# Units 4 to 15 of a recurrence plus gated MLP: outputs, scores and carry in one TensorE visit, on five banks, in a re-searched order

## The chip, the cores and the metric

One core of one Trainium2 chip runs the whole program. The metric is device microseconds of one execution; less is better. The kernel before took 556.14 us (median of three runs, 554.99 to 556.77).

## The reference

A gated linear recurrence over 768 steps for 4 batches of 8 heads with 48 channels each, and then a gated MLP on its output, laid out as 3072 tokens of 384 features (d_ff 1536):

```python
for t in range(S):
    state = alpha[:, :, t, :, None] * state + np.einsum('bhd,bhe->bhde', k[:, :, t], v[:, :, t])
    y[:, :, t] = np.einsum('bhd,bhde->bhe', q[:, :, t], state)
...
g = x @ w_gate
silu = g * (1.0 / (1.0 + np.exp(-g)))
val = x @ w_val
return (silu * val @ w_out).astype(np.float32)
```

## The kernel before

**The recurrence** runs in 16 units of 192 steps, four units to a batch, each of three chunks of 64 steps (`C`, `NU`). The eight heads stand in four groups `g` of two; one head of a group has its channels on partitions 0 to 47, the other on 64 to 111. VectorE scans alpha into decays (`G`, `f`), k and q are scaled by them (`mk`, `q`), and TensorE then does three small jobs per unit, all in f32:

- *scores* (`S`, line 551): k times q inside each chunk, 24 matmuls of 48 rows by 64 columns into two banks. They take turns over all four 64 by 64 quarters of the array: for `f` = 0 rows low to columns high and rows high to columns low, for `f` = 1 low to low and high to high.
- *carry* (`B`, line 575): what each chunk adds to the state, 24 matmuls with 64 rows and 48 columns (16 in the last unit of a batch), all but four of them in one bank. They take turns over two quarters only: rows high to columns low, rows low to columns high.
- *outputs* (`Y`, lines 647, 648 and 664): 36 matmuls, in two banks, 12 over all rows and 24 over quarters. They need the masked scores (`ma`) and the carried states of all chunks (`ad`), which VectorE makes after scores and carry of the same unit.

In the records each of these f32 matmuls is two. For the carry, k is turned to rows by VectorE (`kr`, line 526, eight transposes of 32 by 384 a unit, into one buffer `K`); v is loaded by six DMAs a unit, one for each chunk and parity of head (`V`, line 434); for two of the four groups it is copied once more into `U` (`vc`, line 497). The outputs leave their banks twice: rounded to fp32r on ScalarE (`yh`, line 678) and the rest by VectorE (`yl`, line 682), two of each a unit, and DMAs (`xr`, line 718) put them in the MLP's input `xT`.

**The MLP** runs in eight blocks of 384 tokens, two units to a block, by twelve steps of 128 hidden features: 96 steps `s`, each with a gate product `g`, a value product `v` and an output product `o` of nine matmuls of 128 by 128 by 384 each (lines 733 and 765). `g` has one bank (`gps`), `v` one (`vps`), `o` three (`ops0` to `ops2`). ScalarE takes the gate (`sl`) and rounds (`hh`), VectorE multiplies (`h`), GpSimd or VectorE takes the rest (`hl`). The weights come as 64-bit floats and are cut to f32 pairs by VectorE, ScalarE and GpSimd (`wNv0` to `wNp`) until some 200 us; blocks 0 and 1 are done in two halves of features for that.

**What sets the order:** the string `ORDER`. Each word is an engine letter (t TensorE, v VectorE, s ScalarE, g GpSimd, y the DMA issues of SyncE), a task, and after `@` the banks, by their place in `BANKS` (0 to 2 `A0` to `A2`, 3, 4, 7 `ops0` to `ops2`, 5 `vps`, 6 `gps`). Each engine runs its words in that order; semaphores do the rest. Scores and carry stand side by side; the outputs of the unit before stand next to them in six cases of twelve and elsewhere in the other six.

Of the kernel before, what the change touches and what calls it, by code (L numbers as in the profile page):

```python
# [8 lines left out]
F32 = mybir.dt.float32  # L9
F32R = mybir.dt.float32r  # L10
# [7 lines left out]
P = 128  # L18
# [33 lines left out]
s:x0.0 s:x0.1 s:x0.2 t:Tq2@17 s:cq2 s:w2a g:w2p y:V3.3 y:V2.3 y:wl13 y:V2.5 y:V2.2 y:V2.4 y:Lq3 y:V2.1 v:yl1.0
t:R1.1@2 s:x1.1 v:w4v2 t:Tk2@07 v:mk2 v:f2 t:R1.2@6 t:R1.0@0 s:pk3 s:x1.2 s:x1.0 s:w3a v:w3p v:q2 t:K2.0@4 t:K2.1@7
s:kc2.0 s:kc2.1 t:g0 s:sl0 y:wl5 v:de2 s:w4a t:Tk3@04 t:K2.2@2 s:ea3 t:g1 s:kc2.2 s:qc2 s:sl1 s:w5v0 s:pq3 y:V3.1
v:w4p v:G3 t:v0 v:h0 s:hh0 g:lm0 g:hl0 t:g2 t:C2.0@2 s:ad2.0 t:S2@13 s:sl2 t:C2.1@5 s:ad2.1 v:w5v1 v:mk3 t:Tq3@26
s:cq3 v:f3 t:K3.0@4 g:q3 t:K3.1@7 t:C2.2@0 s:kc3.0 s:kc3.1 s:ad2.2 v:w6v0 t:v1 v:ma2.2 v:lm1 v:ma2.1 v:ma2.0 y:wl12
# [12 lines left out]
y:V5.0 y:os6.1 v:kr4.3 v:kr4.1 v:tq5 t:v13 t:S4@02 t:B4@1 v:w18v0 s:ad4.0 v:h13 y:Lk6 y:V5.4 v:ad4.1 t:o11 t:o12
v:ad4.2 s:hh13 v:qc4 g:hl13 t:g14 v:ma4.0 v:f5 v:ma4.2 v:w16v2 v:w17v1 s:sl14 t:v14 v:h14 t:o13 s:ot13.0 s:ot13.1  # L70
y:os13.1 y:V5.3 y:La6 s:hh14 v:w18v1 v:hl14 v:w18v2 t:g15 s:sl15 t:v15 v:w17v2 s:w16a g:w16p t:g16 v:h15 s:hh15 g:hl15
v:vc4 v:ma4.1 g:q5 s:w17a s:sl16 g:w18a g:w17p y:os13.0 y:wl19 y:pl18.2 y:V5.2 v:kr5.0 t:v16 v:h16 t:g17 s:sl17
v:kr5.1 s:ot13.2 v:tr6 t:v17 t:o14 v:h17 s:hh17 t:Y4@56 g:hl17 g:w18p s:yh4.0 s:w19v0 s:yh4.1 v:tk6 v:kr5.3 v:kr5.2
t:o15 t:S5@10 t:B5@2 v:yl4.1 t:g18 s:sl18 v:yl4.0 v:w19v1 v:G6 v:mk6 v:kr6.2 t:v18 s:hh16 g:hl16 v:w19v2 v:h18 t:g19
s:w19a g:w19p g:qc5 t:o16 s:sl19 s:hh18 g:hl18 v:f6 v:kr6.3 t:v19 v:h19 t:o17 s:hh19 g:hl19 t:o18 t:g20 s:sl20 v:ma5.0
v:de5 v:ma5.1 v:ma5.2 v:ot18.2 y:os13.2 y:wr8 y:Lq6 v:kr6.1 y:xr4.0 y:La7 y:V6.3 y:V6.5 y:xr4.2 v:tq6 y:xr4.1 g:q6
t:v20 v:h20 y:V6.4 y:pl18.1 t:g21 s:hh20 g:hl20 v:ad5.0 v:ad5.1 v:ad5.2 s:vc5 s:sl21 t:v21 v:h21 t:Y5@07 s:yh5.0
y:os18.2 y:V6.1 y:wr19 y:V6.0 y:pl18.0 y:V6.2 y:Lk7 t:g22 v:tr7 y:Lq7 s:yh5.1 s:sl22 v:ot18.1 v:yl5.0 v:kr6.0 v:yl5.1
v:ot18.0 y:xr5.0 y:xr5.1 y:xr5.2 y:os18.0 y:os18.1 t:v22 v:h22 t:S6@21 t:B6@0 t:g23 t:o19 t:o20 s:hh22 g:hl22 v:G7
t:v23 s:hh21 v:f7 v:tk7 v:hl21 t:o21 t:o22 s:sl23 g:mk7 g:qc6 v:h23 v:kr7.1 v:kr7.2 v:kr7.0 v:de6 v:ad6.0 v:ma6.0  # L80
# [101 lines left out]
def main_path(ctx, tc, q, k, v, alpha, w_gate, w_val, w_out, out, flag, spill):  # L182
# [483 lines left out]
    def rows_of(u, i, x):  # L666
        return state[u]["Y"][0:112, x, i::2, :].bitcast(F32R), state[u]["yps"][i][0:112]
# [461 lines left out]
```

## Time and profile before

| | |
|---|---|
| median of three runs | 556.14 us |
| the profiled execution | 557.46 us |
| its span, first to last instruction | 555.6 us |
| granted clock of TensorE, mean | 0.998 |
| busy: TensorE, VectorE, ScalarE, GpSimd | 536.7, 392.0, 253.4, 146.0 us |

Busy time of TensorE counts overlapping records once, and matmuls overlap: one of 337 ns starts 173 ns after the one ahead of it. What a matmul costs the stream is therefore read from the distance between starts, not from its length.

### The profile page before, as it was taken

To read this page: it belongs to the slowest core of one execution; us is meant where nothing else is said; L and a number is where in the kernel's file an instruction comes from. 1 tells how busy PE (TensorE), PEld (TensorE's weight loads), DVE (VectorE), ACT (ScalarE), POOL (GpSimd) and SP (SyncE) were. 2 spreads that over 40 slices of the span, in tenths; PEclk is the share of its full clock that TensorE was granted. 3 is DMA by queue.
4 is the path that set the end of the run, shared out by engine and by line. 5 is a ranking of instruction groups with operands and counts; after the bars stand their busy time and mean duration, and the time that the engine had idled before them with its cause. 6 is when DMAs were issued, how large, how long until landed. Compare 5 with 4: busy or idle time off the path is not lost.

```text
span 555.6 us, 13364 instructions
## 1 busy us (share of the span) xinstructions
PE 536.7 (97%) x5350; PEld 521.0 (94%) x5350; DVE 392.0 (71%) x614; ACT 253.4 (46%) x576; POOL 146.0 (26%) x151
## 2 busy tenths in 40 slices
PE   5899999998999999999999999999999999999996
PEld 4788999998989999999999999999999999999996
DVE  7989998999998997775878559786856332321222
ACT  6888755333223223242332434217243335447775
POOL 7313326626415340112311232142130101001100
PEclk9999999999999999999999999999999999999999
DMA  8979479542576856434247535744361213244453
GB/s 252 267 192 305 134 211 236 148 104 85 148 184 167 196 132 148 109 96 101 75 111 193 136 89 133 154 113 139 90 173 30 67 39 92 81 127 126 127 178 99
DMA packets 95361, 77.59 MB, mean 140 GB/s; under 512 B 32832, under 2 KB 92224, under 8 KB 95296
## 3 DMA queue, kind: packets, MB, share of 16 engines
q1 hardware_dynamic: 95008, 76.32, 51.5%
q8 instruction: 43, 0.70, 0.6%
q10 hardware_dynamic: 288, 0.39, 0.2%
q14 instruction: 22, 0.18, 0.1%
HBM read 62.52 MB, written 5.90 MB: 123 GB/s over the span
## 4 chain that ended last, share of the span: by engine, by line
PE 72%; DVE 13%; DMA 5%; SPq 3%; issue 3%; ACT 2%; POOL 1%; DVEq 0%; ACTq 0%
PE v L733 22%; PE g L733 21%; PE ops L765 20%; DMA L<-in_q_dram 2%; PE y L664 2%; DVE K L526 2%; PE s L551 2%; DVE AT L469 1%; PE A L575 1%; DVE Gs L460 1%; DVE h L745 1%; DVE trk L396 1%; DMA L<-in_alpha_dram 1%; DVE AT L396 1%; PE y L647 1%
## 5 line engine op out<-in xcount | busy, mean ns | idle before, releaser
L733 PE MATMUL v<-xT,w 128*128 128x384 f32 x864 | 167.3, 337 | 2.7 <-DVE h L745 2.7
L733 PE MATMUL g<-xT,w 128*128 128x384 f32 x864 | 167.3, 337 | 0.0
L765 PE MATMUL ops<-w,hh 128*128 128x384 f32 x576 | 157.6, 336 | 0.0
L733 PEld LDWEIGHTS v<-xT,w 128*128 128x128 f32 x864 | 150.7, 188 | 4.8 <-DVE h L745 4.0
L733 PEld LDWEIGHTS g<-xT,w 128*128 128x128 f32 x864 | 150.7, 188 | 1.2 <-ACT xT L708 0.2
L754 POOL TENSOR_TENSOR hl<-h,hh 128x384 fp32r<-128x384 f32 x62 | 63.5, 1028 | 265.9 <-ACT hh L749 248.8
L745 DVE TENSOR_TENSOR h<-h,v 128x384 f32<-128x384 f32 x96 | 53.0, 552 | 101.2 <-PE v L733 97.2
L749 ACT CAST hh<-h 128x384 fp32r<-128x384 f32 x96 | 49.0, 513 | 145.5 <-PE ops L765 76.2
L765 PEld LDWEIGHTS ops<-w,hh 128*128 128x128 f32 x576 | 105.3, 188 | 0.4
L765 PE MATMUL ops<-w,hl 128*128 128x384 f32 x288 | 96.8, 336 | 0.6 <-DVE hl L754 0.6
L741 ACT ACTIVATE h<-g 128x384 f32<-128x384 f32 x96 | 46.9, 489 | 88.1 <-PE g L733 75.8
L526 DVE STREAM_TRANSPOSE K<-Gs 32x384 f32<-32x384 f32 x96 | 54.7, 570 | 2.0
L765 PEld LDWEIGHTS ops<-w,hl 128*128 128x128 f32 x288 | 54.1, 188 | 0.9 <-DVE hl L754 0.9
L754 DVE TENSOR_TENSOR hl<-h,hh 128x384 fp32r<-128x384 f32 x34 | 21.3, 629 | 23.1 <-ACT hh L749 22.9
L344 POOL TENSOR_TENSOR w<-t,w 128x768 fp32r<-128x768 f32 (+1 forms) x13 | 23.4, 1808 | 40.3 <-ACT w L340 36.2
L469 DVE TENSOR_TENSOR_SCAN AT<-AT,back 128x771 f32<-128x771 f32 x16 | 32.9, 2058 | 0.6
L460 DVE TENSOR_TENSOR_SCAN Gs<-AT,inj 128x772 f32<-128x772 f32 x16 | 28.9, 1809 | 0.1
L597 DVE TENSOR_TENSOR X<-s,mask 64x384 f32<-64x384 f32 (+1 forms) x48 | 26.1, 551 | 4.1 <-PE s L551 1.8
L678 ACT CAST X<-y 112x384 fp32r<-112x384 f32 x28 | 12.5, 477 | 27.4 <-PE y L664 21.5
L682 DVE TENSOR_TENSOR X<-y,X 112x384 fp32r<-112x384 f32 x28 | 15.2, 551 | 12.8 <-ACT X L678 12.6
L317 ACT ACTIVATE wc<-wc,wbias 128x384 f32<-128x384 f32 x36 | 23.3, 647 | 1.2
L485 POOL TENSOR_TENSOR X<-trq,AT 112x768 f32<-112x768 f32 x9 | 15.5, 1723 | 22.1 <-DVE K L526 9.8
(122 smaller groups left out, 584.9 us busy)
## 6 DMA issues: line engine op xcount, KB each, us to landing
xT<-X SPq DMA_DIRECT2D x84, 72.0 KB, 2.2
raw<-in_moe_w_gate_dram SPq DMA_DIRECT2D x12, 384.0 KB, 5.1
raw<-in_moe_w_val_dram SPq DMA_DIRECT2D x12, 384.0 KB, 5.2
V<-in_v_dram SPq DMA_DIRECT2D x96, 48.0 KB, 3.7
raw<-in_moe_w_out_dram SPq DMA_DIRECT2D x12, 384.0 KB, 5.6
wc<-in_moe_w_gate_dram SPq DMA_DIRECT2D x12, 384.0 KB, 3.8
wc<-in_moe_w_out_dram SPq DMA_DIRECT2D x12, 384.0 KB, 3.6
wc<-in_moe_w_val_dram SPq DMA_DIRECT2D x12, 384.0 KB, 3.7
```

Source lines behind the costliest of these rows:

```text
L317: nc.scalar.activation(dev, dev, AF.Relu, bias=wbias, scale=-1.0, accum_out=wviol[:, 0, i : i + 1])
L344: eng.tensor_tensor(out=lo, in0=src, in1=hi.bitcast(F32), op=ALU.subtract)
L460: nc.vector.tensor_tensor_scan(*(x.rearrange("p g t -> p (g t)")[:, ::-1] for x in (Gs, AT, inj)), 0.0, op0=ALU.mult, op1=ALU.add)
L469: nc.vector.tensor_tensor_scan(Af, Af, back[:, 1 : n + 1], back[:, 0:1], op0=ALU.mult, op1=ALU.add)
L526: nc.vector.transpose(out=bass.AP(k0.tensor, k0.offset, [k0.ap[0], (G * 2 * D, NU), (2 * D, G), (1, 32)]), in_=Kg[j * BO + x : j * BO + x ...
L597: nc.vector.tensor_tensor(out=X[r, z, f * GF : (f + 1) * GF, :].rearrange("r g (c t) -> r g c t", c=NU), in0=sps[f][r].rearrange("r g (c t ...
L733: nc.tensor.matmul(pt, wsp[kind, f][a][:, kt * P : (kt + 1) * P], xT[blk][:, b_, kt, :], start=(n == 0), stop=(n == 3 * KT - 1),)
L741: nc.scalar.activation(h, acc.pop(("g", blk, f)), AF.Silu)
L745: nc.vector.tensor_tensor(out=h, in0=h, in1=acc.pop(("v", blk, f)), op=ALU.mult)
L749: nc.scalar.copy(out=hh, in_=acc["h", blk, f])
L754: eng.tensor_tensor(out=hl, in0=acc.pop(("h", blk, f)), in1=hh.bitcast(F32), op=ALU.subtract)
L765: nc.tensor.matmul(ops[blk][i], h[b_][:, i * P : (i + 1) * P], wsp["o", f][a], start=(first and n == 0), stop=(last and n == 2),)
```

## The change

The word `Z` takes the place of `S` and `B` for units 4 to 15 and of `Y` for units 4 to 14. `Zu` issues the outputs of unit u-1, the scores of unit u and the carry of unit u, one behind the other (`Z4` has no outputs; `Y15` stays by itself). It holds five banks: one for the outputs of groups 0 and 1, two for the scores, and two (`halves`) that hold the outputs of group 2 or 3 in their first 192 columns and the carry of two groups behind them.

The carry's matmuls now take turns over four quarters, as the scores do: high to low, low to high, high to high, low to low. For that, in groups 2 and 3 the two heads have changed sides in `K` and `V`. v is loaded head by head (eight DMAs a unit in place of six); the transposes of k are halved in width and doubled in number (16 of 32 by 192); the outputs of groups 2 and 3 read `V`, so the copy `vc` is gone from unit 4 on; the outputs are evacuated in three pieces (384, 192 and 192 columns), and a chunk's states (`ad`) in four, where chunks 0 and 1 took two. Units 0 to 3 compute as before. `ORDER` is new on all engines from about unit 0's outputs on.

```diff
 ORDER = """
...
-v:de5 v:ma5.1 v:ma5.2 v:ot18.2 y:os13.2 y:wr8 y:Lq6 v:kr6.1 y:xr4.0 y:La7 y:V6.3 y:V6.5 y:xr4.2 v:tq6 y:xr4.1 g:q6
+t:Z5@12560 s:yh4.0 v:yl4.0 v:ma5.0 v:ma5.1 g:w18p t:v18 g:mk6 v:kr6.0 v:ma5.2 v:h18 v:de5 s:yh4.1 s:yh4.2 v:ad5.0
...
+            g, j = divmod(i, 2)
+            h = j if g >= GF else 1 - j
+            eng.dma_start(
+                out=Vd[h * BO : h * BO + C, :, g, VC[1 - h]],
+                in_=v[b, i, t0 : t0 + T, :].rearrange("(c s) e -> s c e", c=NU),
+            )
...
         for y in range(0, C, 32):
-            r = (1 - j) * BO + y
-            k0 = Kt_[u % NK][r : r + 32, j * D + x : j * D + x + 32]
-            nc.vector.transpose(
-                out=bass.AP(k0.tensor, k0.offset, [k0.ap[0], (G * 2 * D, NU), (2 * D, G), (1, 32)]),
-                in_=Kg[j * BO + x : j * BO + x + 32, :, :, y : y + 32],
-            )
+            for f in range(2):
+                h = j if f else 1 - j
+                r = h * BO + y
+                k0 = Kt_[u % NK][r : r + 32, f * GF * 2 * D + (1 - h) * D + x : f * GF * 2 * D + (1 - h) * D + x + 32]
+                nc.vector.transpose(
+                    out=bass.AP(k0.tensor, k0.offset, [k0.ap[0], (G * 2 * D, NU), (2 * D, GF), (1, 32)]),
+                    in_=Kg[j * BO + x : j * BO + x + 32, :, f * GF : (f + 1) * GF, y : y + 32],
+                )
...
-    def carry(u, bank, whole=False):
+    def carry(u):
...
+        cs = [t_[:, T : T + NU * GF * D].rearrange("p (c g e) -> p c g e", c=NU, g=GF) for t_ in st["halves"]]
+        st["cps"] = [[(slice(f * GF, (f + 1) * GF), cs[f][:, c]) for f in range(2)] for c in range(NU)]
         for c in range(NU - last_of_batch(u)):
...
+            for g0 in range(GF):
+                for f in range(2):
+                    for j in (1, 0) if f else (0, 1):
+                        h = j if f else 1 - j
+                        r, g = slice(h * BO, h * BO + C), f * GF + g0
                         nc.tensor.matmul(
-                            to[j * BO : j * BO + D, g - gs.start, :], Ks[r, x, g, KC[j]], Vd[r, x, g, VC[j]],
-                            start=(x == 0 or not whole), stop=(x == c),
+                            cs[f][j * BO : j * BO + D, c, g0, :], Ks[r, c, g, KC[1 - h]], Vd[r, c, g, VC[1 - h]],
+                            start=True, stop=True,
                         )
...
+            if u >= NROWS:
+                b = [
+                    (to, Vd[r, c, g, cols], X[r, 1, g, cx])
+                    for to, r, cols, g in ((y[E], lo, O, 2), (y[O], up, E, 2), (z[O], lo, O, 3), (z[lo], up, lo, 3))
+                ]
...
+    def burst(u, banks):
+
+
+        halves = [ps.tile([P, 512], F32, tag=banks[i], name=f"c{i}_{u}") for i in range(2)]
+        state[u]["halves"] = halves
+        if banks[4:]:
+            outputs(u - 1, banks[2:3], halves)
+        scores(u, banks[-2:])
+        carry(u)
```

TensorE around unit 9, before. `y_8` are the outputs of unit 8, `s_9` the banks of the scores of unit 9, `A_9` the carry's bank; `g`, `v` and `ops` rows are products of the MLP; x16 is sixteen instructions of one form in a row.

```order
L733 MATMUL v_0_3239<-xT_2680,w_424 128x384 x9
L647 MATMUL y_8_3259<-X_102,V_80 64x64
...
L664 MATMUL y_8_3260<-X_102,V_80 48x64
L733 MATMUL g_1_3324<-xT_2680,w_589 128x384 x9
...
L733 MATMUL g_5_3456<-xT_2680,w_1052 128x384 x9
L551 MATMUL s_9_3486<-X_103,Gs_2943 64x64 x2
L551 MATMUL s_9_3487<-X_103,Gs_2943 64x64 x2
...
L575 MATMUL A_9_3512<-V_81,K_104 48x48 x16
L575 MATMUL s_9_3486<-V_81,K_104 48x48 x4
L575 MATMUL A_9_3512<-V_81,K_104 48x48 x4
L765 MATMUL ops_0_0_3382<-w_964,hh_2_3417 128x384
```

The same place now, with `c_9` for the two `halves`:

```order
L760 MATMUL v_3_3457<-xT_2764,w_967 128x384 x9
L658 MATMUL y_3482<-X_102,V_80 64x64
...
L680 MATMUL c_9_3481<-X_102,V_80 48x64 x2
L680 MATMUL c_9_3480<-X_102,V_80 48x64 x2
L565 MATMUL s_9_3519<-X_103,Gs_3025 64x64 x2
L565 MATMUL s_9_3520<-X_103,Gs_3025 64x64 x2
...
L584 MATMUL c_9_3480<-V_81,K_104 48x48 x2
L584 MATMUL c_9_3481<-V_81,K_104 48x48 x2
...
L760 MATMUL g_4_3577<-xT_2764,w_1088 128x384 x9
```

Two visits between the products have become one, and the carry changes its bank, and with it its quarters, after every two matmuls.

VectorE around the evacuation of unit 6's outputs and unit 8's transposes, before (`h_3` is the MLP's multiplication of step 27):

```order
L682 TENSOR_TENSOR X_102<-y_6_2591,X_102 112x2x192
...
L745 TENSOR_TENSOR h_3_2570<-h_3_2570,v_3_2572 128x384
L597 TENSOR_TENSOR X_103<-s_7_2635,mask 128x384
L682 TENSOR_TENSOR X_102<-y_6_2592,X_102 112x2x192
L526 STREAM_TRANSPOSE K_104<-Gs_2588 32x12x32 x2
L631 SCALAR_TENSOR_TENSOR V_81<-SE,Gs_2366 48x4x48 x2
L625 TENSOR_TENSOR V_81<-A_7_2662,V_81 48x4x48 x2
```

The same place now:

```order
L709 TENSOR_TENSOR X_102<-y_2617,X_102 112x384
L635 SCALAR_TENSOR_TENSOR V_81<-SE,Gs_2349 48x4x48 x2
L472 SCALAR_TENSOR_TENSOR Gs_2742<-AT,inj 128x772
L606 TENSOR_TENSOR X_103<-s_7_2655,mask 128x384
L772 TENSOR_TENSOR h_3_2596<-h_3_2596,v_3_2711 128x384
...
L709 TENSOR_TENSOR X_102<-c_7_2616,X_102 112x192
...
L540 STREAM_TRANSPOSE K_104<-Gs_2742 32x3x2x32 x4
L629 TENSOR_TENSOR V_81<-c_7_2615,V_81 48x2x48 x2
L629 TENSOR_TENSOR V_81<-c_7_2616,V_81 48x2x48 x2
```

A pair of transposes has become four, a pair of state updates two pairs, and the second evacuation two; a scan (`L472`) now stands ahead of `h_3`.

VectorE at the end of the program, before (`vsa` and `oka` belong to the range checks' verdict, `ot` are the last output rows):

```order
L754 TENSOR_TENSOR hl_11_6711<-h_11_6665,hh_11_6696 128x384
...
L801 TENSOR_REDUCE vsa<-viol 128x1
...
L778 COPY ot_1_11_6739<-ops_1_0_6305 128x384
L778 COPY ot_2_11_6742<-ops_2_0_6306 128x192
L945 CAST flag<-cps 1x1
```

The same place now:

```order
L828 TENSOR_REDUCE vsa<-viol 128x1
...
L972 CAST flag<-cps 1x1
L772 TENSOR_TENSOR h_11_6870<-h_11_6870,v_11_6850 128x384
L781 TENSOR_TENSOR hl_11_6893<-h_11_6870,hh_11_6891 128x384
L805 COPY ot_2_11_6907<-ops_2_0_6490 128x192
L805 COPY ot_0_11_6910<-ops_0_0_6488 128x384
```

The verdict has moved ahead of the last multiplication, with its matmul (`cps`) behind the first matmul of step 93's output product on TensorE; and the last copy is now a whole row block (`ot_0`), behind the half one that waits for the last matmul.

## Rows read from the trace of the kernel before

**Rows 1.** The page's first part: busy us, share of the span, instructions

```profile
PE 536.7 (97%) x5350; PEld 521.0 (94%) x5350; DVE 392.0 (71%) x614; ACT 253.4 (46%) x576; POOL 146.0 (26%) x151
```

**Rows 2.** Busy us (instructions) of PE, PEld, DVE, ACT, POOL by stage; clock, DMA

```profile
0.00:36.00 36.00, 25.79 (x437) 21.71 (x438) 31.40 (x51) 27.83 (x64) 17.47 (x36) 1.00 0.82 235
72.00:200.00 128.00, 125.08 (x1219) 121.43 (x1218) 122.04 (x177) 43.76 (x90) 53.57 (x44) 1.00 0.62 162
200.00:440.00 240.00, 239.34 (x2381) 234.71 (x2381) 174.37 (x274) 85.09 (x207) 54.55 (x53) 1.00 0.47 118
440.00:520.00 80.00, 80.00 (x655) 79.23 (x654) 21.12 (x42) 40.88 (x97) 8.95 (x10) 1.00 0.33 93
```

**Rows 3.** Waits of TensorE: us in total, times, longest

```profile
PE pt L416 <- POOL mask L241: 5.1, 1, 5.1
PE v L733 <- DVE h L745: 2.7, 4, 1.8
PE ops L765 <- DVE hl L754: 0.6, 1, 0.6
```

**Rows 4.** Timeline of TensorE, products, then the visit of units 13 and 14 (start, us)

```profile
381.51 1.72 PE L733 MATMUL v<-xT,w 128*128 128x384 f32 x9
383.07 1.72 PE L733 MATMUL g<-xT,w 128*128 128x384 f32 x9
...
392.39 0.34 PE L765 MATMUL ops<-w,hh 128*128 128x384 f32 x1
392.66 0.27 PE L647 MATMUL y<-X,V 128*64 128x64 f32 x1
...
394.22 0.89 PE L551 MATMUL s<-X,Gs 48*64 48x64 f32 x48
394.93 0.91 PE L575 MATMUL A<-V,K 64*48 64x48 f32 x32
...
396.13 1.83 PE L733 MATMUL g<-xT,w 128*128 128x384 f32 x9
397.79 1.94 PE L733 MATMUL v<-xT,w 128*128 128x384 f32 x9
```

**Rows 5.** The same: unit 11's outputs alone, then unit 12's scores and carry

```profile
340.19 0.34 PE L765 MATMUL ops<-w,hh 128*128 128x384 f32 x1
340.46 0.27 PE L647 MATMUL y<-X,V 128*64 128x64 f32 x1
...
342.15 1.84 PE L733 MATMUL g<-xT,w 128*128 128x384 f32 x9
343.82 0.34 PE L765 MATMUL ops<-w,hh 128*128 128x384 f32 x1
...
351.72 0.93 PE L551 MATMUL s<-X,Gs 48*64 48x64 f32 x48
352.47 0.89 PE L575 MATMUL A<-V,K 64*48 64x48 f32 x32
...
353.64 0.44 PE L765 MATMUL ops<-w,hh 128*128 128x384 f32 x1
```

**Rows 6.** VectorE by line and form: xcount, busy us, mean ns, idle before

```profile
L526 DVE STREAM_TRANSPOSE K<-Gs 32x384 f32<-32x384 f32 x96 | 54.7, 570 | 2.0
L682 DVE TENSOR_TENSOR X<-y,X 112x384 fp32r<-112x384 f32 x28 | 15.2, 551 | 12.8 <-ACT X L678 12.6
L625 DVE TENSOR_TENSOR V<-A,V 48x192 f32<-48x192 f32 x42 | 14.8, 353 | 1.0
L625 DVE TENSOR_TENSOR SE<-A,V 48x96 f32<-48x96 f32 x18 | 4.6, 255 | 0.3
L497 DVE COPY U<-V 64x288 f32<-64x288 f32 x2 | 0.7, 352 | 0.0
```

**Rows 7.** Timeline of VectorE and ScalarE (q: its DMA issue) at the end

```profile
550.13 0.85 DVE L778 COPY ot<-ops 128x384 f32<-128x384 f32 x2
551.36 0.34 ACTq L786 DMA_DIRECT2D out_dram<-ot  x1
```

**Rows 8.** The v loads: xcount, ns of one issue min/median/max

```profile
L434 SPq DMA_DIRECT2D V<-in_v_dram x96: 595/612/1172, 6.4 to 437.9; - x96
```

More of the change, by code (lines that the diff above doesn't have):

```diff
@@ L52 @@
[L52 to L56, printed above, removed]
@@ L612, in advance @@
             return
-        if st["whole"] and c == 0:
-            for j in range(2):
-                r = slice(j * BO, j * BO + D)
-                (eng.copy if eng is nc.scalar else eng.tensor_copy)(out=Vd[r, 1:NU, :, VC[j]], in_=st["both"][r])
-            return
         for gs, cps in st["cps"][c]:
@@ L621, in advance @@
                 to = Vd[r, c + 1, gs, VC[j]] if c + 1 < NU else SE[r, gs]
-                if st["whole"] or c == 0 and first_of_batch(u):
+                if c == 0 and first_of_batch(u):
                     (eng.copy if eng is nc.scalar else eng.tensor_copy)(out=to, in_=cps[r])
@@ L634, in decay, with outputs @@
             )
-    def outputs(u, banks):
+    def outputs(u, banks, halves=None):
         st = state[u]
         X, Vd = st["X"], st["V"]
-        st["yps"] = [ps.tile([P, 2, T], F32, tag=banks[i], name=f"y{i}_{u}") for i in range(2)]
-        y, z = (t_[:, 1, :] for t_ in st["yps"])
+        if halves is None:
+            yps = [ps.tile([P, 2, T], F32, tag=banks[i], name=f"y{i}_{u}") for i in range(2)]
+            st["yps"] = [(slice(i, G, 2), yps[i][0:112]) for i in range(2)]
+            y, z = (t_[:, 1, :] for t_ in yps)
+            early = [yps[g][:, 0, :] for g in range(GF)]
+        else:
+            yf = ps.tile([P, GF, T], F32, tag=banks[0], name=f"y_{u}")
+            early = [yf[:, g, :] for g in range(GF)]
+            z, y = (t_[:, 0:T] for t_ in halves)
+            st["yps"] = [(slice(0, GF), yf[0:112]), (2, y[0:112]), (3, z[0:112])]
         lo, up, E, O = slice(0, BO), slice(BO, P), slice(0, D), slice(BO, BO + D)
@@ L645, in outputs @@
             for g in range(GF):
-                yps = st["yps"][g]
-                nc.tensor.matmul(yps[lo, 0, cx], Vd[:, c, g, lo], X[:, 0, g, cx], start=True, stop=True)
-                nc.tensor.matmul(yps[O, 0, cx], Vd[0:112, c, g, O], X[0:112, 1, g, cx], start=True, stop=True)
+                nc.tensor.matmul(early[g][lo, cx], Vd[:, c, g, lo], X[:, 0, g, cx], start=True, stop=True)
+                nc.tensor.matmul(early[g][O, cx], Vd[0:112, c, g, O], X[0:112, 1, g, cx], start=True, stop=True)
         for c in range(NU):
@@ L664, in outputs @@
                     nc.tensor.matmul(to[:, cx], w_, x_, start=first, stop=second)
+    def burst(u, banks):
[5 more added lines that the diff above has]
+        carry(u)
     def rows_of(u, i, x):
[L667 removed]
+        gs, yps = state[u]["yps"][i]
+        return state[u]["Y"][0:112, x, gs, :].bitcast(F32R), yps
     def rows_hi(u, i):
@@ L821, in named_unit @@
             todo[f"L{nm}{u}"] = lambda eng, nm=nm: load_u(u, nm)
-        for i in range(2 * NU):
+        for i in range(2 * NU if u < NROWS else H):
             todo[f"V{u}.{i}"] = lambda eng, i=i: load_v(u, i, eng)
@@ L858, in named_unit @@
         todo[f"mk{u}"] = mk
-        for i in range(2):
+        for i in range(3 if NROWS <= u < nun - 1 else 2):
             todo[f"yh{u}.{i}"] = lambda eng, i=i: rows_hi(u, i)
@@ L878, in named_unit @@
         todo[f"S{u}"] = lambda eng, *banks: scores(u, banks)
-        todo[f"B{u}"] = lambda eng, bank: carry(u, bank)
+        todo[f"Z{u}"] = lambda eng, *banks: burst(u, banks)
         for c in range(NU):
```

206 lines of the change are left out of this document (101 added, 105 removed).

## The prediction

> **What bounds the kernel now.** First the page's busy shares [rows 1]: TensorE is busy 97% of the span, VectorE 71%, the rest far less. Then the stages [rows 2], since the share is an average: to 36 us TensorE is busy 25.8 us, from 72 to 200 us 125.1 of 128, and from 200 to 520 us 319.3 of 320. So behind 200 us every microsecond taken from TensorE's stream shortens the program, unless something new makes it wait. From 72 to 200 us VectorE is busy 122.0 of 128, only 6.0 us short of full; behind 200 us it is at 73% and then 26%. Then what TensorE waited for [rows 3]: once 5.1 us for the mask at the start, and for VectorE's `h` and `hl` 3.3 us in all. There is hardly a wait to remove; the change can only make the stream itself shorter. What the stream spends on the units is read from distances between starts: nine products take 383.07 - 381.51 = 1.56 us, 0.173 each, and the visit of units 13 and 14 goes 392.66 (outputs), 394.22 (scores), 394.93 (carry), 396.13 (products): 1.56, 0.71 and 1.20 us [rows 4]. Scores and carry are 48 records each, the carry's with 48 moving columns where the scores have 64, and yet a score costs 14.8 ns and a carry 25.0 ns. The scores go round four quarters of the array and two banks, the carry round two quarters and, mostly, one bank. This difference is what I expect most of the gain from.
>
> **The carry.** It takes the scores' pattern. Bounds: nothing gained, 25.0 ns; and the scores' cost in proportion to the moving columns, 14.8 x 48/64 = 11.1 ns, so 0.53 us a unit. If it costs what a score costs, 0.71 us. The pattern is the scores' own and there are fewer columns, so I take a little under that, 0.65: a saving of 0.55 us in the nine units with 48 records, and of two thirds of it, 0.36, in the three (7, 11, 15) that have 32. 9 x 0.55 + 3 x 0.36 = 6.0 us; at 0.71 it is 5.4, at 0.53 it is 7.4, at 25.0 ns nothing.
>
> Against this stands a rule of the Trainium skill ("TensorE: Matmul & The Clock Gate", section "Wait — 56ns, not 53.3ns?"): starts of matmuls never come closer than about 25 ns, however few columns they have. The carry before stands just on it, and by it this term would be zero and the sum the first rival's. The 14.8 ns of the scores [rows 4] are below it on this chip, so I give it little.
>
> **Fewer visits.** Going into the small matmuls and out of them costs. Unit 11's outputs alone begin 0.27 us after the product ahead started, where the stream's step is 0.17 (0.10 lost); they take 342.15 - 340.46 = 1.69 where they took 1.56 with scores behind them (0.13); and the nine products behind take 1.67, not 1.56 (0.11) [rows 4, 5]. Unit 12's scores and carry by themselves take 0.75 + 1.17, about what they take in the joint visit (1.91). Joining two visits therefore saves 0.34 us. Before, units 4 to 15 had 18 visits (12 of scores and carry, 12 of outputs, six of them joint); now 12 `Z` and `Y15`, 13. 5 x 0.34 = 1.7 us. This has one answer, give or take 0.2.
>
> **What it adds on VectorE.** Per unit 16 transposes of 192 in place of eight of 384 at 570 ns. No row shows the half; between 285 ns (in proportion) and 570 I take 365, because a tensor operation of 192 columns takes 353 ns where one of 384 takes 551, 0.64 of it [rows 6]: 16 x 0.365 - 8 x 0.570 = +1.28 us. State updates: twelve pieces of 96 at 255 ns for four of 192 and four of 96: 3.06 - 2.43 = +0.63. Evacuation: 551 + 2 x 353 for 2 x 551: +0.16. Together +2.1 us a unit; behind 200 us it lies beside TensorE's work in VectorE's 27% idle time and costs nothing. Units 4, 5 and 6 fall into the full stage: +6.2 us. Taken off there: one copy of v (2 x 0.35), and by the new order two weight steps fewer of about half to one us each on balance; I count +4.4. Against the 6.0 us idle this fits, but only with next to no gap left, and VectorE's queue is in order: `h` behind four transposes is `v`'s bank not free. In this stage TensorE should gain 3 x 0.55 + 2 x 0.34 = 2.3 us; I take 1.5 of it as given back to waits for `h`, and for the range from 0 to 4.4 us.
>
> **Banks and waits.** `Z` needs five banks at once and all inputs of three jobs. The outputs of a unit or its scores often sit in `vps` or `gps`, the bank of the next product but one. The cover: the outputs are done 0.71 + 0.65 = 1.36 us ahead of the visit's end, the scores 0.65 us, and at least one product of 1.56 us comes between, against one or two pieces of 551 ns and a ScalarE copy. Most visits have that; I take 0.5 us for the few with VectorE scans in between, and 0 to 1.5 for the range.
>
> **Loads, copies, start.** 24 more v loads at 0.61 us of SyncE's issue [rows 8], 14.7 us spread over 400: nobody on the path waits for SyncE now, so nothing; if an `xr` store queued behind them comes late, TensorE waits up to the 1.2 us of two issues once. The third ScalarE copy a unit and the copies of v dropped on ScalarE and GpSimd are off the path: nothing. The start is reordered behind unit 0's outputs, with the same matmuls; TensorE is free 10 us there, half of it before the mask [rows 2, 3]. Transposes of later units now stand in gaps ahead of carries that wait for copies: -0.3, between -1.5 and +1.5.
>
> **The end.** Before, VectorE's last two copies run together (0.85 us) and the last store is issued at 551.36 [rows 7]. Now the half block waits for the last matmul and the whole block (0.55) runs behind it, and the two stores queue behind that: +0.5. The verdict's matmul now stands inside step 93's output product; if its chain of small VectorE operations comes late, TensorE waits there; bounded by one product, 1.56. I take +0.3.
>
> **Sum.** -6.0 - 1.7 - 0.3 + 1.5 + 0.5 + 0.5 + 0.3 = -5.2 us. The profiled execution took 557.46 (span 555.6), so it would take 552.3; it stands 1.3 above the median of the runs shown, and from the median, 556.14, the forecast is 551.0. Its own range is 548 to 554.4.
>
> **Rivals.**
> 1. *The carry gains nothing*, since its spacing is a floor of instructions and not of quarters. For it: 25 ns in both places where two quarters are used. Against it: the scores' 14.8. Then +0.8: 557. 5%.
> 2. *VectorE becomes the bound, and it is slower.* The mechanism is the half transposes in the stage to 200 us: if one costs as much as a whole one, 570 ns, units 4 to 6 need 48 x 0.205 = 9.8 us more there. VectorE then needs 122.0 + 4.4 + 9.8 = 136.2 us in a stage of 128: 8.2 us later, where the sum has the stage 0.8 sooner; 551 + 9 = 560. It starts to bite at (6.0 - 4.4)/48 + 0.365 = 0.40 us a transpose. Against it: fixed parts of some 150 ns in the operations of [rows 6]. 5%.
> 3. *Bank hand-over.* Each of the eleven joint visits is followed by half a microsecond of waiting for evacuations: +5.5 in place of +0.5, 556. For it: five of eight banks in one hand and `g` and `v` with a bank each; against it: the covers above. 8%.
> 4. *Nothing is given back*: the carry at 0.53 us, VectorE's load absorbed: -7.4 - 1.7 - 0.3 + 1.0 = -8.4, 547.7. 15%.
>
> That the change does not do what it says is excluded by the order: one visit, and a bank that changes every two matmuls.
>
> **How the numbers follow.** About 0.3% (1.7 us) is what a measurement of this kernel can tell from no change, so faster means under 554.5, slower over 557.8. Forecast 67% and rival 4 15%: faster 0.82. Rivals 1 and 3: mostly the same, 0.12. Rival 2 and the upper edge of rival 1: slower, 0.06. Range: 546 to 555.5; below lies an even better start with rival 4, above lie rivals 1 to 3.
>
> **What would show it.** The carry's line with 48 records between its start and the first product 0.53 to 0.71 us apart, not 1.2. Thirteen visits from unit 4 on, with 1.56 + 0.71 + 0.65 us inside. Transposes near 365 ns. VectorE over 125 of 128 us in the stage to 200 us, and TensorE's waits for `h` there some 1.5 us above 3; none of note behind 200 us; the first 36 us as before. I am wrong if the carry stays near 25 ns, if transposes stay over 0.4 us, or if TensorE's waits rise by more than 5 us, whoever ends them.

## The result, and the profile after

The changed kernel takes 549.04 us (median of four executions, 548.65 to 551.06), the kernel before beside it 555.58: a ratio of 0.989, interval 0.986 to 0.991. Measured again later on one chip with other kernels it was 549.52 us and 0.986, interval 0.983 to 0.989. Forecast were 551.0 us, faster, in a range of 546.0 to 555.5. The profiled execution took 549.33 us (span 547.6), 8.1 us less than that of before.

The page's first part, answering [rows 1]; then the stages (us; busy us and instructions of PE, PEld, DVE, ACT, POOL; clock, DMA share, GB/s), answering [rows 2]; then what is left of TensorE's waits for VectorE's `h`, answering [rows 3] (it is the one at unit 10, behind 200 us):

```profile
PE 529.1 (97%) x5350; PEld 514.7 (94%) x5350; DVE 400.3 (73%) x755; ACT 249.8 (46%) x579; POOL 152.3 (28%) x149
```

```profile
0.00:36.00 36.00, 26.12 (x438) 21.50 (x439) 32.60 (x52) 27.88 (x63) 20.16 (x38) 1.00 0.87 248
72.00:200.00 128.00, 127.43 (x1249) 124.49 (x1248) 123.28 (x226) 44.84 (x92) 54.30 (x43) 1.00 0.59 153
200.00:440.00 240.00, 238.35 (x2405) 235.38 (x2404) 178.74 (x353) 96.16 (x240) 51.91 (x46) 1.00 0.51 130
440.00:520.00 80.00, 80.00 (x658) 79.23 (x657) 26.02 (x59) 41.67 (x101) 10.87 (x12) 1.00 0.37 110
```

```profile
PE y L658 <- DVE h L772: 1.2, 1, 1.2
```

VectorE has 141 instructions more and only 8.3 us more to do; in the stage to 200 us it is 1.2 us more, where I had added 4.4, and TensorE is busier there (127.4 us for 125.1).

The visit of units 8 and 9 on TensorE, answering [rows 4] (start, us):

```profile
251.26 0.27 PE L658 MATMUL y<-X,V 128*64 128x64 f32 x1
...
252.82 0.90 PE L565 MATMUL s<-X,Gs 48*64 48x64 f32 x48
253.52 0.74 PE L584 MATMUL c<-V,K 64*48 64x48 f32 x48
254.19 1.83 PE L760 MATMUL g<-xT,w 128*128 128x384 f32 x9
255.86 1.38 PE L760 MATMUL v<-xT,w 128*128 128x384 f32 x7
```

Outputs 1.56 us, scores 0.70, carry 0.67, and the nine products behind it 1.67 where nine in the stream take 1.56. In [rows 4] the carry took 1.20.

VectorE by line and form, answering [rows 6]: the half transposes, the state updates, the evacuation (x count | busy us, mean ns | idle before):

```profile
L540 DVE STREAM_TRANSPOSE K<-Gs 32x192 f32<-32x192 f32 x192 | 71.1, 370 | 3.3
L629 DVE TENSOR_TENSOR V<-c,V 48x96 f32<-48x96 f32 x84 | 21.4, 255 | 2.8 <-ACT V L627 0.5
L709 DVE TENSOR_TENSOR X<-c,X 112x192 fp32r<-112x192 f32 x22 | 7.4, 351 | 0.3
```

Where the 8 us lie I read from distances between starts on TensorE. From the first output product on both kernels have the same 2538 products; a product's step is 0.173 us, and what exceeds it is a wait or an exit from small matmuls.

| | before | after | difference |
|---|---|---|---|
| start of the first output product | 55.5 us | 55.8 | +0.3 |
| small matmuls behind it, entries and waits inside included | 45.8 | 41.1 | -4.7 |
| products over their step, 72 to 200 us | 5.5 | 2.4 | -3.1 |
| products over their step, the rest | 3.7 | 2.3 | -1.4 |
| last product's start to the end | 5.4 | 6.2 | +0.8 |

So there are two gains of similar size: the visits, as forecast (4.7 us, and 0.6 us of exits among the products), and waits between products that went away (3.9 us), which I had not forecast.

### The profile page after: what moved, and what is told of

It reads as the page before. It is cut to its first block, busy times and chain, and to the rows that moved or that the text cites. A ratio compares the mean times of both kernels' runs of the same rounds, so it can differ in the third digit from the quotient of the medians.

```text
span 547.6 us, 13551 instructions
## 1 busy us (share of the span) xinstructions
PE 529.1 (97%) x5350; PEld 514.7 (94%) x5350; DVE 400.3 (73%) x755; ACT 249.8 (46%) x579; POOL 152.3 (28%) x149
## 4 chain that ended last, share of the span: by engine, by line
PE 83%; DVE 7%; DMA 3%; SPq 2%; issue 1%; ACT 1%; POOL 0%; DVEq 0%; POOLq 0%
PE v L760 25%; PE ops L792 25%; PE g L760 25%; DMA L<-in_q_dram 3%; PE s L565 2%; PE c L680 2%; DVE K L540 1%; PE c L584 1%; PE y L658 1%; DVE AT L481 1%; PE y L659 1%; SPq L456 1%; DVE Gs L472 1%; DVE trq L399 1%; DMA V<-in_v_dram 1%
## 5 line engine op out<-in xcount | busy, mean ns | idle before, releaser
L781 POOL TENSOR_TENSOR hl<-h,hh 128x384 fp32r<-128x384 f32 x65 | 70.5, 1085 | 283.5 <-ACT hh L776 274.7
L540 DVE STREAM_TRANSPOSE K<-Gs 32x192 f32<-32x192 f32 x192 | 71.1, 370 | 3.3
L347 POOL TENSOR_TENSOR w<-t,w 128x768 fp32r<-128x768 f32 (+1 forms) x15 | 27.5, 1839 | 35.1 <-ACT w L343 26.1
L781 DVE TENSOR_TENSOR hl<-h,hh 128x384 fp32r<-128x384 f32 x31 | 18.5, 596 | 23.5 <-ACT hh L776 23.3
L481 DVE TENSOR_TENSOR_SCAN AT<-AT,back 128x771 f32<-128x771 f32 x16 | 29.2, 1824 | 0.6
L472 DVE TENSOR_TENSOR_SCAN Gs<-AT,inj 128x772 f32<-128x772 f32 x16 | 28.9, 1806 | 0.4 <-ACT AT L856 0.2
L497 POOL TENSOR_TENSOR X<-trq,AT 112x768 f32<-112x768 f32 x11 | 18.7, 1700 | 30.9 <-DMA xT<-X 8.5
L629 DVE TENSOR_TENSOR V<-c,V 48x96 f32<-48x96 f32 x84 | 21.4, 255 | 2.8 <-ACT V L627 0.5
L883 POOL TENSOR_TENSOR Gs<-trk,Gs 128x768 f32<-128x768 f32 x9 | 15.3, 1701 | 25.8 <-DVE Gs L472 22.0
```

Of the source, the lines that this page charges most:

```text
L347: eng.tensor_tensor(out=lo, in0=src, in1=hi.bitcast(F32), op=ALU.subtract)
L472: nc.vector.tensor_tensor_scan(*(x.rearrange("p g t -> p (g t)")[:, ::-1] for x in (Gs, AT, inj)), 0.0, op0=ALU.mult, op1=ALU.add)
L481: nc.vector.tensor_tensor_scan(Af, Af, back[:, 1 : n + 1], back[:, 0:1], op0=ALU.mult, op1=ALU.add)
L540: nc.vector.transpose(out=bass.AP(k0.tensor, k0.offset, [k0.ap[0], (G * 2 * D, NU), (2 * D, GF), (1, 32)]), in_=Kg[j * BO + x : j * BO + x ...
L781: eng.tensor_tensor(out=hl, in0=acc.pop(("h", blk, f)), in1=hh.bitcast(F32), op=ALU.subtract)
```

## The carry: quarters or banks

Three kernels take the carry apart, and the kernel after is the fourth arrangement. First, the inner loops exchanged:

```diff
-            for g0 in range(GF):
-                for f in range(2):
+            for f in range(2):
+                for g0 in range(GF):
```

> The kernel after with the carry's two inner loops exchanged: the same 24 matmuls into the same banks, but four in a row now stay in one pair of quarters and in one bank. If quarters or banks in turn make the carry cheap, both are undone: 25 ns a record as before the change, 1.20 us a unit with 48 records where it is 0.65 to 0.68, so 9 x 0.55 + 3 x 0.36 = 6.0 us more than the kernel after: 555.0 us, a ratio to before of 0.999. If the gain is somewhere else (fewer visits, the order alone), the carry stays near 0.66 us or its price does not reach the end: 549 us, 0.988.

Measured: 549.52 us, ratio 0.986 (0.980 to 0.992), carry 0.74 us a unit. My arithmetic for it was wrong: two quarters for four matmuls in a row are nearly as good as four in turn. So two quarters had to be held for longer. With `f` outermost, twelve matmuls in a row stay in one pair of quarters and one bank:

```diff
-        for c in range(NU - last_of_batch(u)):
-            for g0 in range(GF):
-                for f in range(2):
+        for f in range(2):
+            for c in range(NU - last_of_batch(u)):
+                for g0 in range(GF):
```

> The kernel after with the carry's outer loop over the pair of groups: twelve matmuls in a row in one pair of quarters and one bank, then twelve in the other pair and the other bank. Theory of a quarter that is taken for 90 ns by each matmul, with the next ones let in behind it only in order: four in a row still overlapped with the next four (0.74 us a unit in the run with exchanged inner loops), twelve in a row hardly do, 24 x 45 + 0.1 = 1.1 to 1.2 us a unit, 554 to 555 us, ratio 0.998. If the way round the quarters does not matter, and the price has gone down for another reason (operands in V and K, the place in the visit), 0.66 to 0.74 us and 549 to 550 us, 0.988 to 0.99.

Measured: 553.41 us, ratio 0.994 (0.991 to 0.996). Banks are told from quarters by one more, two quarters throughout and two banks in turn:

```diff
...
-                    for j in (1, 0) if f else (0, 1):
-                        h = j if f else 1 - j
+                    for j in range(2):
+                        h = 1 - j
...
-                            cs[f][j * BO : j * BO + D, c, g0, :], Ks[r, c, g, KC[1 - h]], Vd[r, c, g, VC[1 - h]],
+                            to[c][f][j * BO : j * BO + D, g0, :], Ks[r, c, g, KC[1 - h]], Vd[r, c, g, VC[1 - h]],
```

> The kernel after, with the carry's matmuls of the groups 2 and 3 sent through the two quarters of the groups 0 and 1 (high to low, low to high), alternating after every two matmuls between the bank of the groups 0 and 1 and free columns in a bank of the scores: two quarters only, two banks in turn. It leaves out the state of groups 2 and 3 (what is computed for them there is read by nobody, and they take over the other groups' piece). The number of matmuls, their columns and the evacuations are those of the kernel after. Theory of quarters: a quarter takes one f32 matmul of 48 columns in 90 ns (before: two quarters, 49 ns from one matmul to the next), so 24 of them take 1.18 us a unit where four quarters take 0.66: 5.7 us more than the kernel after, 554.7 us, ratio to before 0.999. Theory of banks: the bank's change is what counts, 0.66 to 0.74 us a unit and 549 us, 0.988.

Measured: 555.95 us, ratio 0.997 (0.995 to 0.999). Unit 9's carry on TensorE in this run (`c` and `s` are the two banks in turn), then in the run with twelve in a row:

```profile
258.76 0.28 PE L586 MATMUL c<-V,K 64*48 64x48 f32 x4
258.85 0.28 PE L586 MATMUL s<-V,K 64*48 64x48 f32 x4
258.94 0.28 PE L586 MATMUL c<-V,K 64*48 64x48 f32 x4
...
259.75 0.28 PE L586 MATMUL s<-V,K 64*48 64x48 f32 x4
259.96 1.83 PE L762 MATMUL g<-xT,w 128*128 128x384 f32 x9
```

```profile
254.43 1.14 PE L584 MATMUL c<-V,K 64*48 64x48 f32 x48
255.50 1.86 PE L760 MATMUL g<-xT,w 128*128 128x384 f32 x9
```

A row of the first fence is four records, two matmuls, one in each quarter; the next row starts 0.09 us later, whichever bank it writes. So a matmul of this size (f32, 64 rows, 48 columns) holds its quarter for about 90 ns. Reckon a carry as rounds of 90 ns and 0.11 us for the way out, and let a matmul wait in order until its quarter is free; the measured times are those of visits without a wait. Four quarters in turn: six rounds, 0.65 us (measured 0.65 to 0.68). Four in a row: each second round of one pair overlaps the first of the other, seven rounds, 0.74 (0.72 to 0.75). Twelve in a row: eleven rounds, 1.10 (1.05 to 1.08). Two quarters only: twelve, 1.19 (1.18 to 1.20). These two numbers give all four within 0.05 us. Changing the bank did not help two quarters. What one bank would do to four quarters is not shown: in that arrangement, and in the one with four matmuls in a row and the bank in turn, matmuls of the two row halves write the same partitions of a bank with nothing to order them, so neither has a time. In time, the whole change without the cheap carry is worth 0.3% and with it 1.1 to 1.4%.

The 25 ns between starts, which the prediction weighed as a floor for any matmul (the Trainium skill, "TensorE: Matmul & The Clock Gate", section "Wait — 56ns, not 53.3ns?"), is none here: 48 records in 0.67 us are 14 ns each.

## A visit's price

Outputs issued one product ahead of scores and carry, for ten units, so ten visits more. For unit 9 (`P` is the new word, and `Z9`, a product later, issues what is left):

```diff
-t:o38 t:v39 s:sl39
+t:o38 s:sl39 t:P9@206 t:v39
```

> The kernel after with the outputs of ten units (5 to 9 and 11 to 15) issued one product earlier than scores and carry, so ten more visits, with the same matmuls and banks. The prediction's price of a visit is 0.34 us: 3.4 us more than the kernel after, 552.4 us, ratio to before 0.994. Rival: going into the small matmuls and out of them is hidden or costs only the 0.1 us of the entry: 549 to 550 us, 0.988 to 0.990.

Measured: 561.49 us, ratio 1.006 (1.003 to 1.010); 12 us above the 549.52 of the run with exchanged loops beside it, not 3.4. Where neither visit waits, the step's price holds: outputs 1.79 us, scores and carry 1.51, each with its entry of some 0.1 in it and 0.11 more on the products behind, against 3.04 and 0.11 for the joint visit: 0.37 us. The other 8 us are waits, most of them for a bank that ScalarE's gate or VectorE's `h` has yet to free (unit 9, us):

```profile
254.75 0.33 PE L566 MATMUL s<-X,Gs 48*64 48x64 f32 x4
255.53 0.86 PE L566 MATMUL s<-X,Gs 48*64 48x64 f32 x42 [0.46 <-DVE h L778]
```

## VectorE: how near the bound, and where

The transposes of k issued twice, for three units in the full stage and then, in another kernel, for three behind it (9, 10 and 11):

```diff
-            for f in range(2):
+            for f in (0, 1) * (2 if u in (4, 5, 6) else 1):
```

> The kernel after with the 16 transposes of k of the units 4, 5 and 6 issued twice (the second writes the same values again): 48 x 0.37 = 17.8 us more of VectorE between 85 and 160 us. Theory that VectorE is near its limit in the stage from 72 to 200 us, as the prediction's second rival had it: 4.7 us are idle there, so 17.8 - 4.7 = 13 us longer; with queues that run ahead 8 to 13, ratio to before 1.003 to 1.012. Rival, that the stage has more room than its idle time shows (work that can wait, since only the multiplications h and the states are urgent): under 4 us, ratio under 0.996.

Measured: 571.84 us, ratio 1.027 (1.023 to 1.032): 22 us over the kernel after, more than the 17.8 us of work. Part of it is TensorE's clock: its waits grow to 3.8 us, and the granted clock, 1.00 throughout this stage in the kernel after, is 0.83, 0.85, 0.83 and 0.88 in the ten microseconds from 100, 120, 150 and 170 us. By these means some 6 us of full clock (2.4 GHz) are lost, an estimate; the 16 us that are left are near the work, and over both theories.

> The kernel after with the transposes of k of the units 9, 10 and 11 issued twice: the same 17.8 us more for VectorE as in the run with units 4 to 6 (which cost 22 us), but from 205 to 300 us, where VectorE is busy 75% and TensorE 99%. The prediction's step, that VectorE's added work behind 200 us lies beside TensorE's and costs nothing: 549 to 551 us, ratio to before 0.986 to 0.989. Rival, that VectorE's queue in order is what matters wherever it stands (a multiplication behind four to eight more transposes is 1.5 to 3 us late): 2 to 6 us longer, 0.992 to 0.998.

Measured: 565.64 us, ratio 1.015 (1.011 to 1.018): 16 us, in a stage where VectorE has a quarter of its time free; both theories were far off. TensorE's waits in it (us in total, times, longest):

```profile
PE c L584 <- DVE K L540: 4.5, 2, 4.2
PE v L760 <- DVE h L772: 4.1, 4, 1.9
PE y L658 <- DVE h L772: 2.6, 2, 1.5
```

Unit 11's carry waits 4.2 us for its own transposes, and products wait for an `h` that stands behind others. VectorE ahead of such a product (start, us), and the stretch around it:

```profile
243.24 3.13 DVE L540 STREAM_TRANSPOSE K<-Gs 32x192 f32<-32x192 f32 x8
246.41 0.55 DVE L772 TENSOR_TENSOR h<-h,v 128x384 f32<-128x384 f32 x1
```

```profile
240.00:250.00 10.00, 7.58 (x35) 6.94 (x34) 9.38 (x19) 3.21 (x9) 3.71 (x3) 0.87 0.28 76
```

The granted clock is 0.87 there, 0.96 in the next ten microseconds and 0.83 from 310 to 320 us: some 3.4 of the 16 us by the same estimate. Idle time of an in-order engine is therefore not by itself room for more work. Even the searched order shows this once, at unit 10: its visit waits for `h` of step 44, which stands behind a scan (VectorE, then TensorE):

```profile
276.53 1.82 DVE L481 TENSOR_TENSOR_SCAN AT<-AT,back 128x771 f32<-128x771 f32 x1
...
278.52 0.56 DVE L772 TENSOR_TENSOR h<-h,v 128x384 f32<-128x384 f32 x1
```

```profile
279.13 0.27 PE L658 MATMUL y<-X,V 128*64 128x64 f32 x1 [1.25 <-DVE h L772]
```

This and three other places were mended, beside the kernel after:

```diff
-v:f6 t:o16 t:g19 s:sl19 v:kr5.1 v:kr5.0
+v:kr5.1 v:kr5.0 v:f6 t:o16 t:g19 s:sl19
-v:f11 v:h44
+v:h44 v:f11
-y:Lk15 y:os59.2 y:V14.6 g:q14 y:V14.2 y:V14.4
+y:V14.6 y:V14.2 y:V14.4 y:Lk15 y:os59.2 g:q14
-v:ot95.2 s:oh v:ot95.0
+v:ot95.0 v:ot95.2 s:oh
```

> The kernel after, beside the three below on the same chip: 0.986 to 0.991 of before.

> The kernel after with ORDER mended at the four places where its trace shows TensorE waiting in or behind a visit: VectorE's multiplication of step 44 ahead of a scan of unit 11 (the wait of 1.3 us at 277.5 us), unit 14's last three v loads ahead of the k load of unit 15 on SyncE (0.67 us inside the carry at 393 us), unit 5's last two transposes of K ahead of a scan of unit 6 (0.41 us at 138.7 us), and at the end the whole row block's copy ahead of the half one (0.3 to 0.5 us). Theory that these waits are what the five banks and the new order cost: 2.0 to 2.9 us less than the kernel after, ratio to it 0.995 to 0.996. Rival: what is taken from one wait comes back at the next (the scan that is pushed back holds up another multiplication): within 0.5 us of the kernel after.

Measured: the kernel after 549.52 us, 0.986; this one 551.48, 0.991 (0.988 to 0.995): no gain. Unit 10's visit is 0.4 to 0.8 us shorter and the end 0.45; the loads moved at unit 14 changed nothing there; and the scan moved behind unit 5's transposes now holds up the evacuation there, for 1.9 us where 0.4 were lost:

```profile
141.62 2.15 PE L760 MATMUL v<-xT,w 128*128 128x384 f32 x9 [1.87 <-DVE X L709]
```

Behind this wait the granted clock is 0.50, 1.2 GHz, from 143 to 146 us, and the products lose some 1.6 us more. That wait and its clock outweigh what the other places gave back.

## Why waits went away: VectorE beside GpSimd

Comparing means by line in the two traces shows something that I had not looked for: the same operations are shorter after the change (the second scan, a weight cut, the decay of the state). Before, then after:

```profile
L469 DVE TENSOR_TENSOR_SCAN AT<-AT,back 128x771 f32<-128x771 f32 x16 | 32.9, 2058 | 0.6
L164 DVE SCALAR_TENSOR_TENSOR t<-raw,t 128x768 uint32<-128x768 uint32 x12 | 13.5, 1129 | 0.1
L631 DVE SCALAR_TENSOR_TENSOR V<-SE,Gs 48x192 f32<-48x192 f32 x24 | 10.5, 438 | 0.5
```

```profile
L481 DVE TENSOR_TENSOR_SCAN AT<-AT,back 128x771 f32<-128x771 f32 x16 | 29.2, 1824 | 0.6
L164 DVE SCALAR_TENSOR_TENSOR t<-raw,t 128x768 uint32<-128x768 uint32 x14 | 13.3, 952 | 0.1
L635 DVE SCALAR_TENSOR_TENSOR V<-SE,Gs 48x192 f32<-48x192 f32 x24 | 8.6, 359 | 0.3
```

Summed over all operations, the time over the shortest of each form is 26.8 us before, 11.2 of it between 72 and 200 us; after, 16.0 and 3.7. The longest case of before is behind TensorE's largest wait for `h` in [rows 3] (GpSimd, VectorE, TensorE):

```profile
123.20 2.15 POOL L344 TENSOR_TENSOR w<-t,w 128x768 fp32r<-128x768 f32 x1 [7.50 <-ACT w L340]
```

```profile
123.59 2.58 DVE L164 SCALAR_TENSOR_TENSOR t<-raw,t 128x768 uint32<-128x768 uint32 x1
126.10 0.54 DVE L745 TENSOR_TENSOR h<-h,v 128x384 f32<-128x384 f32 x1
```

```profile
126.69 0.62 PE L733 MATMUL v<-xT,w 128*128 128x384 f32 x2 [1.76 <-DVE h L745]
```

The cut starts during GpSimd's subtraction, which ends at 125.35; from there it is 0.8 us to its end, where the same operation alone takes 0.95. It stood still for some 1.6 us. A pair of kernels tests what GpSimd must do for that, with work for GpSimd whose result nobody reads:

```diff
         eng.tensor_tensor(out=hl, in0=acc.pop(("h", blk, f)), in1=hh.bitcast(F32), op=ALU.subtract)
+        if eng is nc.gpsimd and (blk, f) in early:
...
+            for _ in range(2):
+                eng.tensor_tensor(out=spare, in0=inj.rearrange(...)[:, 0:336], in1=inj.rearrange(...)[:, 336:672], op=ALU.mult)
```

and in the twin, at the same place, five times `eng.memset(spare, 0.0)`.

> The kernel after, and behind each of GpSimd's subtractions hl of the steps 5 to 23 two more GpSimd multiplications of 336 columns, whose inputs are a constant tile and whose result nobody reads: some 17 x 2 x 0.95 = 32 us more for GpSimd from 85 to 200 us, where it is busy 54 of 128 us. Theory of collisions: VectorE's operations on two SBUF inputs (scans, weight cuts, multiplications of decays) stand still or stretch while GpSimd reads SBUF, and the old order lost 11.2 us of VectorE's time to that between 72 and 200 us, the new one 3.7. Then VectorE's time in this stage grows by 8 us or more, over the 4.7 us that are idle, and the kernel takes 3 to 10 us longer: 552 to 559 us. Theory of GpSimd's queue alone: 0 to 3 us, as much as the twin that only writes, and VectorE's mean durations stay.

> The twin: at the same places five GpSimd fills (memset) of the same 336 columns, some 2 us together, which read nothing from SBUF. They hold up GpSimd's queue as the multiplications do. Theory of collisions over SBUF reads: VectorE's durations stay as in the kernel after (3.7 us of stretching between 72 and 200 us), and the time is 549 to 551 us, what the delay of hl costs. Theory that any GpSimd work slows VectorE: as the twin that reads.

Measured: 567.38 us with reads, ratio 1.019 (1.015 to 1.024); 564.80 with fills, 1.014 (1.011 to 1.017). VectorE from 72 to 200 us, the second scan and a weight operation, with reads and then with fills:

```profile
L481 DVE TENSOR_TENSOR_SCAN AT<-AT,back 128x771 f32<-128x771 f32 x4 | 8.5, 2132 | 0.2
L347 DVE TENSOR_TENSOR w<-t,w 128x768 fp32r<-128x768 f32 x2 | 2.6, 1302 | 0.0
```

```profile
L481 DVE TENSOR_TENSOR_SCAN AT<-AT,back 128x771 f32<-128x771 f32 x4 | 7.3, 1824 | 0.2
L347 DVE TENSOR_TENSOR w<-t,w 128x768 fp32r<-128x768 f32 x2 | 1.9, 946 | 0.0
```

The same operations at the same places are longer beside reads and not beside fills: in all 9.8 us over the shortest in this stage against 5.0, where the kernel after has 3.7. This is what the Trainium skill states ("SBUF — State Buffer", section "Who interferes with whom"): a VectorE instruction with two SBUF inputs and a GpSimd instruction that reads SBUF block each other, the later one until the earlier ends. In time, though, both theories were far off: some 15 of the 18 us come with fills alone, from GpSimd's own queue being late (`hl`, `mk`, the weights), though with the fills it is busy only 81 of 128 us here. Reads add 2.6 us to that, but they also kept GpSimd busy for 5.4 us more than the fills (37.6 us against 32.2), and the two intervals overlap: the stretched operations are shown, their price in time is not.

Does the kernel before get back the wait when a collision is taken away? Two words moved in the order before, and in another kernel the colliding operation given to VectorE:

```diff
-v:w17v2 s:w16a g:w16p t:g16 v:h15
+s:w16a g:w16p t:g16 v:h15 v:w17v2
-v:hl21
+g:hl21
```

> The kernel before, all of it, with two words of ORDER moved: the last step of weight group 17 on VectorE behind the multiplication of step 15 (it stood ahead of it, and took 2.58 us where its like take 0.95, while GpSimd worked on a weight group), and the subtraction hl of step 21 on GpSimd, ahead of the decay's multiplication there (on VectorE it took 1.65 us where 0.55 is usual, beside that same multiplication). Theory of collisions: TensorE's waits of 1.9 us at 124.6 and of 0.7 us at 170.1 us go, and the kernel takes 2 to 2.6 us less, ratio to before 0.995 to 0.9965; so much of what the change brought would be an accident of the order before. Rival: VectorE has so little idle time in this stage that the wait comes back at the next multiplication: 0 to 0.5 us, 0.999 to 1.

```diff
-v:w17v2 s:w16a g:w16p t:g16 v:h15
+v:w17v2 s:w16a t:g16 v:h15 v:w16p
```

> The kernel before, with one operation moved: the low part of weight group 16, on GpSimd 2.15 us from 123.20 us on, is done by VectorE behind the multiplication of step 15 (0.95 us there). GpSimd then reads nothing while VectorE does the last cut of weight group 17. Theory of collisions: that cut takes 0.95 us where it took 2.58, the multiplication behind it ends 1.55 us sooner, and TensorE's wait of 1.9 us at 124.6 us falls to 0.2 to 0.4; VectorE has 0.7 us less to do in all. The kernel takes 1.3 to 1.9 us less, ratio to before 0.9965 to 0.9977. Rival: the copies of v behind it now meet GpSimd's next operations, as in the run with two moves, and a wait of 2 us or more comes back within 5 us: no gain, or up to 6 us longer.

Measured: 563.64 us, ratio 1.011 (1.008 to 1.015), and 561.29, 1.009 (1.005 to 1.013). Both slower, by 6 and 4 us. In the second the cut takes 0.95 us as expected, and the next VectorE operation, the copies of v (0.72 us for two before), meet GpSimd operations in a row. VectorE, GpSimd and TensorE there:

```profile
122.76 0.95 DVE L164 SCALAR_TENSOR_TENSOR t<-raw,t 128x768 uint32<-128x768 uint32 x1
...
125.08 5.27 DVE L497 COPY U<-V 64x288 f32<-64x288 f32 x2
```

```profile
125.89 1.72 POOL L485 TENSOR_TENSOR X<-trq,AT 112x768 f32<-112x768 f32 x1
127.56 0.82 POOL L340 CAST w<-t 128x768 fp32r<-128x768 f32 x1
128.34 1.80 POOL L344 TENSOR_TENSOR w<-t,w 128x768 fp32r<-128x768 f32 x1
```

```profile
132.73 3.02 PE L733 MATMUL v<-xT,w 128*128 128x384 f32 x9 [4.97 <-DVE h L745]
```

So in the second the rival held, and the first lies outside both of its theories: one collision taken away lets a worse one in, and TensorE waits 5.0 us where it had waited 1.8. The wait has a second price. In the run with two moves it is 4.5 us long, and TensorE's granted clock (third last number) is at half speed, 1.2 GHz, behind it:

```profile
125.00:132.00 7.00, 2.50 (x13) 1.86 (x12) 6.90 (x6) 2.08 (x4) 5.44 (x4) 1.00 0.39 120
132.00:136.00 4.00, 2.96 (x9) 2.96 (x10) 3.67 (x5) 0.00 (x0) 0.00 (x0) 0.50 0.00 0
136.00:140.00 4.00, 4.00 (x42) 3.58 (x45) 3.58 (x5) 0.51 (x1) 0.29 (x1) 0.64 0.01 4
```

Nine products take 3.25 us there, where 1.7 to 1.8 is usual. Shown, then: collisions make TensorE wait, for up to 5 us at a time, and in the full stage the new order has a third of the old one's time over the shortest (3.7 us of 11.2). Not shown: that all 3.1 us by which the products' loss fell there come from this; no run takes the collisions out of the old order and leaves the rest.

## Point by point against the prediction

- **Carry, -6.0.** Measured 9 x 0.52 + 3 x 0.36, -5.8. Right in mechanism and size: the quarters carry it in the runs above. Its rival, the floor, fell. The half transposes (365 ns taken, 370 measured) and the pieces of 96 and 192 columns were right too.
- **Fewer visits, -1.7.** Five fewer at 0.37: -1.9.
- **VectorE's give-back, +1.5.** This step failed. What the products lose over their step fell by 3.9 us, exits not counted, where I had it rise by 1.5. I added the new operations to VectorE's busy time and compared the sum with the idle time, and took the durations in that busy time for fixed. They held 11.2 us over the shortest of their forms, visible as operations of one line that differ twofold; in the new order it is 3.7. The added work itself I had too small: with 1.2 us more busy time and 7.5 less of this, some 8.7 us of work came into the stage where I counted 4.4, since the transposes of more than four units lie in it (68 pieces), not of three. So VectorE did not come over the 125 us that I had named as a sign, and the waits for `h` went away where I had 1.5 us more. The second rival's condition, slow transposes, did not come; its mechanism (VectorE as the bound) is real, since three units' transposes once more cost 22 us.
- **"Behind 200 us it costs nothing."** True of this order, false as a reason: the same work there, not searched for, cost 16 us.
- **Bank hand-overs, +0.5.** Waits inside visits rose by 2.1 us: 1.3 at unit 10, 0.5 at unit 5 (transposes of K), 0.7 at unit 14 and 0.1 elsewhere, less 0.5 at unit 9 of the kernel before. The third rival's mechanism, once and not eleven times.
- **Start, -0.3.** +0.3. But the first output product starts between 54.4 and 58.3 us in the fourteen traces, whose code is nearly the same up to there; this term cannot be told from chance.
- **The end, +0.5 and +0.3.** +0.8 and +0.2: the whole row block is copied behind the half one, and the two stores go out together (compare [rows 7]):

```profile
541.77 0.82 DVE L805 COPY ot<-ops 128x192 f32<-128x192 f32 x2 [1.97 <-PE ops L792]
```

```profile
542.63 0.87 ACTq L813 DMA_DIRECT2D out_dram<-ot  x2
```

The sum of the measured terms, -5.8 - 1.9 + 0.3 - 3.9 + 2.1 + 0.8 + 0.2, is -8.2, with rounding the 8.1 us between the profiled executions; mine was -5.2. The forecast held because the large term was right and the failed one, 5.4 us off, was partly met by waits inside visits and the rest; that the misses partly cancelled is luck.

## What to carry over

Send small f32 matmuls round all four quarters of the array: each of 48 columns holds its quarter for some 90 ns, and changing the bank did not help where only two quarters took turns. In a stage where an engine is full, look at how far operations of one form differ before adding to their sum: what stands still there beside another engine moves with the order, here by 7.5 us where the work added was 8.7. A wait of TensorE can cost twice, by itself and by the clock behind it. Idle time of an in-order engine is not free room by itself; put new work where its own due time and that of the work behind it allow, or search the order again.

## What was not expected of the hardware

- A VectorE copy of 64 by 288 (352 ns alone) took 4.2 us beside three GpSimd operations that followed one another without a gap: it ended 0.2 us behind the last of them. The run with two moves has the same (4.18 us). The copy has one SBUF input; two were not needed for this collision.
- TensorE's granted clock fell to 0.50 (1.2 GHz) behind a wait of 4.5 us, and also behind one of 1.9 us in the run with four places mended; it stayed at 1.00 behind the wait of 1.8 us in the kernel before. The length of the wait alone does not tell these runs apart.
- GpSimd, busy 42% of the stage, was late for TensorE as soon as 32 us were added to its queue: with the fills TensorE waits 4.9 us for its results (`q`, `hl`, a weight group), in the kernel after not at all behind the start.
